# Chunked attention and a softplus FFN on one core: the first four blocks' q and k read in runs of 8 tokens and turned by 64x64 products, with a new order of tasks

## The chip, the cores and the metric

One core of one Trainium2 chip runs the whole program. The metric is the device time of one execution in microseconds. Three executions of the kernel before give a median of 824.95 us (824.27 to 824.95).

## The reference

The inputs q, k, v have the shape (8 batches, 8 heads, 576 tokens, 64) in float32; w_in (512 x 2048) and w_out (2048 x 512) are stored in 8 bytes an element. Attention runs inside chunks of 64 tokens; the heads are then joined into 4608 rows of 512 and go through a two-layer network with softplus.

```
scores = scale * np.matmul(q_c, k_c.transpose(0, 1, 2, 4, 3))   # per chunk of 64 tokens
scores = scores - np.max(scores, axis=-1, keepdims=True)
attn = np.exp(scores)
attn = attn / (np.sum(attn, axis=-1, keepdims=True) + 1e-09)
out = np.matmul(attn, v_c)
...
x = np.ascontiguousarray(attn_out.transpose(0, 2, 1, 3)).reshape(B * S, H * D)
h = x @ w_in
g = np.maximum(h, 0.0) + np.log1p(np.exp(-np.abs(h)))
return (g @ w_out).astype(np.float32)
```

## The kernel before

The tokens are cut into 36 blocks of 128 tokens (two chunks, all 8 heads) and into 9 groups of 512 tokens (four blocks). The program treats the groups in two ways. The first three go straight through: GEMM1 with w_in, softplus, GEMM2 with w_out. The other six go in pairs through a scheme with fewer products (`product`, `mix`, `f_product`); that part begins at about 310 us, and the change leaves its code alone.

Each matrix product is made of three float32r products: a high and a low part of each operand, without low times low. So every weight tile is decoded first. `w_load` brings 512 KB of raw words into one of three buffers, `w_top` and `w_low` take it apart (ScalarE or GpSimd), `w_add` joins the pieces (VectorE), `w_hi` rounds (ScalarE or GpSimd) and `w_lo` subtracts (VectorE or GpSimd). There are 32 such units, called by their number: `w_add3` is the join of unit 3. They are needed one pair per step of GEMM1 and GEMM2 until about 95 us.

The first four blocks (`FIRST_BLK = 4`) open the program, since nothing else can start before their attention. For block i the tasks are, in the names that the planner uses:

- `q{i}`, `k{i}`, `v{i}` (`pe_load`): one DMA each on SyncE's queue; token s goes to partition s, with 8 heads of 64 numbers beside each other, so each piece of 256 bytes is a packet of its own.
- `T{i}` (`pe_t`): 4 transposes of 128x128 for q and 4 for k on TensorE, each with two heads, into two PSUM tiles. `tq{i}` and `tk{i}` copy them to SBUF, both on ScalarE.
- `S{i}` (`pe_s`): scores, 16 products of 64x64; rows and output of one head lie in the same half of the partitions, and heads alternate between the halves.
- `max{i}` on VectorE, `sub{i}` on TensorE (`pe_sub`: adds minus the maximum into PSUM by one product with 512 columns), `exp{i}` on ScalarE, `den{i}` on VectorE (three instructions), `norm{i}` on VectorE, or on GpSimd for blocks 0 and 3.
- `E{i}` transposes the result (4 transposes), `ec{i}` copies it, `V{i}` multiplies by v, `xh{i}` (ScalarE) and `xl{i}` (VectorE) split it into the high and low part of x.

GEMM1 of the first two steps is cut in halves: `G1_a0` and `G1_a1` use blocks 0 and 1, `G1_0` and `G1_1` blocks 2 and 3. With these come `spa0` (softplus), `hia0`, `loa0`, `G2_a0` and so on. Later blocks run as bursts between the GEMM steps; their q and k are loaded in other layouts and turned on VectorE (`blk_t4`, tasks `Uq4`, `Tq4`, ...).

TensorE is kept busy while it waits by filler products of the identity with itself (`keep_warm`); their number comes from the gap that the planner expects. The order of work is made in two steps. `Plan.order` makes a schedule from costs, due times and pool sizes. `Plan.emit` takes each engine's list from it, moves tasks to other engines (`MOVED`), puts single tasks behind others (`BEHIND`), and writes out the program. Each engine then works through its own list in that order, and stalls where the next instruction's input isn't there. A DMA that is issued is an instruction in its queue's list too.

Of the kernel before, what the change touches and what calls it, by code (L numbers as in the profile page):

```python
# [33 lines left out]
class Plan:  # L34
# [108 lines left out]
            raise ValueError(f"never ready: {[n for n in T if n not in fin][:12]}")  # L143
        return out, fin

    def emit(self, moved=(), behind=(), around=lambda t: t["fn"]()):
        T, out = self.tasks, self.order()[0]
        start, lanes, gaps, last = {}, {}, {}, 0.0
        for now, t in out:
# [5 lines left out]
        for name, change in moved:  # L155
            if "eng" in change:
                lanes[T[name]["eng"]].remove(name)
                lanes[change["eng"]].append(name)
            T[name].update(change)
        for name, other in behind:  # L160
            lane = lanes[T[name]["eng"]]
            lane.remove(name)
            lane.insert(lane.index(other) + 1, name)
            gaps[name] = gaps[other] = 0.0
# [27 lines left out]
def chunked_attention_softplus_ffn(  # L192
# [193 lines left out]
    def hd(t):  # L386
        return t.rearrange("p (h d) -> p h d", d=D)
# [39 lines left out]
    def pe_t(i):  # L427
        if i < 2:
            tq, tk = (po_tile(n) for n in range(2))
        else:  # L430
            pa = pa_tile()
            tq, tk = pa[:, 0, :], pa[:, 1, :]
        keep_warm(tq)
        for dst, n in ((tq, 0), (tk, 1)):
            src = hd(slot(i, n))
            for hp in range(HP):
                nc.tensor.transpose(
                    dst[:, hp * P : (hp + 1) * P], src[:, 2 * hp : 2 * hp + 2, :], ident
                )
        live["t", i] = tq, tk  # L440

    def pe_tq(i):
        nc.scalar.copy(slot(i, 3), live["t", i][0])

    def pe_tk(i):
        copy = nc.scalar.copy if i not in TK else nc.vector.tensor_copy
        copy(slot(i, 4), live["t", i][1])

    def pe_s(i):
# [182 lines left out]

    def att_norm(i):
        e, den = live["e", i], live.pop(("den", i))
        (nc.gpsimd if i in NORM_POOL else nc.vector).tensor_tensor(
            e, e, den.unsqueeze(3).to_broadcast(list(e.shape)), op=ALU.mult
        )

# [447 lines left out]

    SOLO = {"a0": 1, "a1": 2}
    HALVED = {"a0": (0, 0), "0": (0, 1), "a1": (1, 0), "1": (1, 1)}
    MOVED = [("w_hi1", {"eng": "ACT"}), ("lo0", {"eng": "DVE"}), ("lo1", {"eng": "DVE"}), ("G1_a0", {"take": []}), ("G1_a1", {"take": []})]
    for fc in range(2):  # L1090
        a, b = f"a{fc}", str(fc)
        MOVED += [(f"sp{a}", {"take": [("u", [f"lo{a}", f"lo{b}"])]}), (f"sp{b}", {"take": []})]
        MOVED += [(f"hi{a}", {"take": [("g", [f"G2_{a}", f"G2_{b}"])]}), (f"hi{b}", {"take": []})]
    BEHIND = (
# [7 lines left out]
    )  # L1102
    plan = Plan(raw=RAW_BUFS, top=TOP_BUFS, low=LOW_BUFS, po0=1, po1=1, po2=1, po3=1, pa=2, g=LAG + 1, u=1,
                ws=1, out0=1, out1=1, out2=1, out3=1, ring0=1, ring1=1, ring2=1, other0=1, other1=1, other2=1, uu0=1, uu1=1, ux0=1, ux1=1)
# [611 lines left out]
                reason="one engine at a time on the memory port",  # L1716
            )

    plan.emit(MOVED, BEHIND, in_turn)


# [32 lines left out]
```

## Time and profile before

| | |
|---|---|
| three executions | 824.95 us median, 824.27 to 824.95 |
| the profiled execution | 824.5 us |
| its span, first to last instruction | 822.7 us |
| TensorE busy | 811.7 us, 99% of the span |
| VectorE busy | 566.0 us, 69% |
| ScalarE busy | 390.9 us, 48% |
| GpSimd busy | 406.3 us, 49% |

All times in the rows are microseconds from the start of the span, unless ns is marked. PE is TensorE, DVE is VectorE, ACT is ScalarE, POOL is GpSimd, SPq is SyncE's queue. A float32 product stands in the trace as two instructions (passes), a transpose or a float32r product as one: `x32` at line 459 are the 16 products of one `S`. The profiled execution took 0.45 us less than the median of the three.

### The profile page before, as it was taken

The numbers are of one execution on the slowest core, as the hardware profiler recorded it, in microseconds if no ns is written. First come the engines' busy times: TensorE is split into PE (matmuls) and PEld (weight loads), VectorE is DVE, ScalarE is ACT, GpSimd is POOL, SyncE is SP. The second block draws the span as 40 slices with busy tenths as digits, with TensorE's granted clock in tenths as the row PEclk, the third lists the DMA queues.
The fourth block names the chain that finished last, engine by engine and source line by source line (L and its number), as shares of the span: only waits on it lengthen the run. The fifth ranks groups of instructions, "written<-read, shape, count | busy, mean of one in ns | idle before, by whom it ended". The sixth has DMA issues, their size and how long they took to land.

```text
span 822.7 us, 16614 instructions
## 1 busy us (share of the span) xinstructions
PE 811.7 (99%) x6186; PEld 686.3 (83%) x6186; DVE 566.0 (69%) x914; ACT 390.9 (48%) x635; POOL 406.3 (49%) x512
## 2 busy tenths in 40 slices
PE   9999999999999999999999999999999999999997
PEld 7787888888888888888888777888888887999997
DVE  3998985357556687386779787376784635798773
ACT  4877765444543574354346444363541424443431
POOL 1555569686987743868856564337204550000000
PEclk9999999999999999999999999999999999999999
DMA  9887767763474456899897499896529999963421
GB/s 217 241 213 199 210 161 220 222 155 112 87 192 124 110 153 215 224 261 253 213 228 186 111 340 288 230 246 209 178 95 315 330 329 342 388 224 115 144 78 52
DMA packets 216483, 168.90 MB, mean 205 GB/s; under 512 B 153937, under 2 KB 186705, under 8 KB 215505
## 3 DMA queue, kind: packets, MB, share of 16 engines
q1 hardware_dynamic: 201648, 117.75, 49.7%
q0 software_dynamic: 14208, 49.56, 20.0%
q8 instruction: 49, 0.80, 0.4%
q10 hardware_dynamic: 544, 0.52, 0.2%
q14 instruction: 34, 0.27, 0.1%
HBM read 115.87 MB, written 50.86 MB: 203 GB/s over the span
## 4 chain that ended last, share of the span: by engine, by line
PE 74%; DMA 10%; DVE 6%; ACT 3%; POOL 3%; issue 3%; SPq 1%; DVEq 0%; ACTq 0%; POOLq 0%
PE po L917 25%; PE pa L858 16%; PE pa L685 13%; PE pa L1060 8%; PE po L1060 6%; DMA spill<-ends 3%; PE pa L648 2%; PE pa L560 1%; DMA raw<-spill 1%; PE po L858 1%; DVE wib L884 1%; DMA xb<-scratch 1%; DMA raw<-in_q_dram 1%; DMA raw<-in_moe_w_out_dram 1%; DVE wib L340 1%
## 5 line engine op out<-in xcount | busy, mean ns | idle before, releaser
L917 PE MATMUL po<-late,g_hi 128*128 128x512 f32 x360 | 110.4, 393 | 0.0
L858 PE MATMUL pa<-wib,xb 128*128 128x512 f32 x360 | 86.8, 394 | 0.7 <-DMA xb<-scratch 0.5
L858 PEld LDWEIGHTS pa<-wib,xb 128*128 128x128 f32 x360 | 66.0, 188 | 19.2 <-ACT wib L864 3.4
L917 PEld LDWEIGHTS po<-late,g_hi 128*128 128x128 f32 x360 | 66.7, 188 | 14.6 <-DVE late L371 0.4
L858 PE MATMUL pa<-wi_hi,xb 128*128 128x512 f32 x240 | 74.3, 390 | 0.8 <-ACT wib L864 0.6
L917 PE MATMUL po<-wo_hi,g_hi 128*128 128x512 f32 x192 | 72.1, 394 | 0.0
L917 PE MATMUL po<-wo_hi,g_lo 128*128 128x512 f32 x192 | 71.4, 391 | 0.2 <-DVE g_lo L709 0.2
L917 PE MATMUL po<-wo_lo,g_hi 128*128 128x512 f32 x192 | 71.2, 390 | 0.0
L917 PE MATMUL po<-late,g_lo 128*128 128x512 f32 x192 | 70.9, 389 | 0.0
L701 ACT ACTIVATE u<-pa 128x512 f32<-128x512 f32 (+1 forms) x48 | 28.3, 589 | 82.1 <-PE pa L685 76.4
L813 POOL DMA_DIRECT2D xb<-scratch x58 | 36.0, 621 | 59.2 <-PE pa L858 57.7
L884 DVE TENSOR_TENSOR wib<-wib,pa 128x512 f32<-128x512 f32 x64 | 44.0, 688 | 26.9 <-PE pa L858 14.5
L892 ACT ACTIVATE ends<-pa 128x512 f32<-128x512 f32 x40 | 23.9, 599 | 76.8 <-PE pa L858 32.2
L858 PEld LDWEIGHTS pa<-wi_hi,xb 128*128 128x128 f32 x240 | 45.0, 188 | 10.9 <-ACT wib L864 1.1
L884 POOL TENSOR_TENSOR wib<-wib 128x512 f32<-128x512 f32 x32 | 42.0, 1312 | 19.5 <-ACT wib L864 19.0
L584 DVE STREAM_TRANSPOSE eT<-qe 32x256 f32<-32x256 f32 x112 | 48.8, 436 | 2.6
L884 DVE TENSOR_TENSOR wib<-pa,wib 128x512 f32<-128x512 f32 x24 | 16.6, 692 | 49.1 <-ACT ends L892 31.4
L864 ACT COPY wib<-pa 128x512 f32<-128x512 f32 x52 | 28.7, 587 | 40.9 <-PE pa L858 40.9
L685 PE MATMUL pa<-xb,wib 128*128 128x512 f32 x192 | 46.5, 390 | 0.3 <-DVE wib L371 0.2
L858 PE MATMUL pa<-wi_lo,xb 128*128 128x512 f32 x120 | 46.7, 389 | 0.0
L709 POOL TENSOR_TENSOR g_lo<-u,g_hi 128x512 fp32r<-128x512 f32 x23 | 31.0, 1348 | 24.7 <-ACT g_hi L705 21.9
L917 PEld LDWEIGHTS po<-wo_hi,g_lo 128*128 128x128 f32 x192 | 36.0, 188 | 8.6 <-DVE g_lo L709 1.1
(370 smaller groups left out, 2078.0 us busy)
## 6 DMA issues: line engine op xcount, KB each, us to landing
xb<-scratch POOLq DMA_DIRECT2D x38, 512.0 KB, 5.4
spill<-ends SPq DMA_DIRECT2D x35, 512.0 KB, 4.8
xb<-scratch POOLq DMA_DIRECT2D x20, 768.0 KB, 6.5
ends<-spill SPq DMA_DIRECT2D x21, 512.0 KB, 3.3
out_dram<-raw SPq DMA_DIRECT2D x34, 256.0 KB, 3.5
raw<-in_moe_w_in_dram SPq DMA_DIRECT2D x16, 512.0 KB, 5.0
raw<-in_moe_w_out_dram SPq DMA_DIRECT2D x16, 512.0 KB, 4.6
scratch<-ends SPq DMA_DIRECT2D x16, 512.0 KB, 2.9
```

Source lines behind the costliest of these rows:

```text
L584: nc.vector.transpose(live["eT", i][d : d + BL, tb], e[s : s + BL, 1 - tb])
L648: nc.tensor.matmul(pa[o, a, col : col + C], vt[r, 4 * j + 2 * h2 + c2, :], eT[r, :, 4 * c2 + 2 * j + h2, :], start=True, stop=True,)
L685: nc.tensor.matmul(ph, wt[:, c, :], x[:, ts_, c, :], start=(n == 0), stop=(n == 3 * KC - 1))
L701: nc.scalar.activation(w["u"], w["ph"], AF.Softplus)
L709: (nc.gpsimd if pool else nc.vector).tensor_tensor(w["lo"], w["u"], w["hi"].bitcast(F32), op=ALU.subtract)
L813: on("ring").dma_start(to[:, here], src[:, cut])
L858: nc.tensor.matmul(w["bank"][BANK[k]], wts[:, q, c, :], x[:, c, :], start=k < NX and c + n == 0, stop=c == 1 and n == 2, skip_group_check= ...
L864: nc.scalar.copy(tmp_of(n), w["bank"][n])
L884: (nc.gpsimd if what in MIX_POOL and w["s"] < LAST else nc.vector).tensor_tensor(out, a, b, op=op)
L892: nc.scalar.activation(u_tiles(j)[i], src, AF.Softplus)
L917: nc.tensor.matmul(pos[w["m"]][t], terms[n][0][:, j * P : (j + 1) * P], terms[n][1], start=(w["first"] and n == 0), stop=n == 2 and w["last"],
L1060: nc.tensor.matmul(f_bank(k)[:, t * HW : (t + 1) * HW], x[:, t * P : (t + 1) * P], wt, start=j == n == t == 0, stop=j == 7 and n == 2 and ...
```

## The change

It has four parts.

1. Loads. For q and k of the first four blocks, 8 tokens of one head that follow each other (2048 bytes) become one piece on one partition. A partition holds one head and one group of 8 tokens; even heads lie in partitions 0 to 63, odd heads in 64 to 127, and within a half the group index is outermost. Each load becomes two DMAs of 64 partitions. All of k0 to k3 is issued by ScalarE, q0 to q3 by SyncE.
2. Turning. For each of the 8 token offsets in a run and each half, one plain 64x64 product of the data with the identity writes 64 columns that lie 8 apart in the PSUM tile: 16 products for q and 16 for k of a block, in place of 4 and 4 transposes.
3. Engines. `tk0`, `tk1`, `norm0` and the subtractions `sub0`, `sub1` go to VectorE (the subtractions then write the result to SBUF).
4. Order. The five engines' opening lists are written out (`FIRST`), with 6 filler products ahead of `T0` (`WARM`) and 1 ahead of `S0`. The list `BEHIND` is another one. On TensorE nothing behind `G1_4` changes except two steps of GEMM1 at about 120 us, which now stand ahead of two steps of GEMM2; ScalarE, VectorE and GpSimd have single tasks swapped with a neighbour over the whole run.

```diff
 def pe_load(eng, i, src, n):
+    if n < 2:
+        (_, rows, b, s0), = rows_of(i)
+        for h2 in range(2):
+            eng.dma_start(
+                slot(i, n)[h2 * C : (h2 + 1) * C],
+                src[b, h2::2, s0 : s0 + rows, :].rearrange("h (g r) d -> g h (r d)", r=RUN),
+            )
+        return
...
     for dst, n in ((tq, 0), (tk, 1)):
-        src = hd(slot(i, n))
-        for hp in range(HP):
-            nc.tensor.transpose(
-                dst[:, hp * P : (hp + 1) * P], src[:, 2 * hp : 2 * hp + 2, :], ident
-            )
+        src = slot(i, n).rearrange("p (r d) -> p r d", r=RUN)
+        dst = dst.rearrange("p (h g r) -> p g h r", h=HP, r=RUN)
+        for run in range(RUN):
+            for a in range(2):
+                r = slice(a * C, (a + 1) * C)
+                nc.tensor.matmul(dst[r, :, :, run], src[r, run, :], ident[r, r], start=True, stop=True)
...
+    MOVED = [("w_hi1", {"eng": "ACT"})] + [(n, {"eng": "DVE"}) for n in ("lo0", "lo1", "tk0", "tk1", "norm0")]
+    MOVED += [(f"sub{i}", {"eng": "DVE", "fn": partial(att_sub, i)}) for i in range(2)]
+    MOVED += [(f"S{i}", {"take": [(f"po{2 + i}", [f"sub{i}"])]}) for i in range(2)]
+    MOVED += [(f"k{i}", {"eng": "ACT", "fn": partial(pe_load, nc.scalar, i, k, 1)}) for i in range(FIRST_BLK)]
...
+        "PE": (
+            "T0 S0 T1 T2 S1 E0 S2 T3 V0 sub2 E1 S3 V1 sub3 E2 G1_a0 V2 G1_a1 E3 V3 G2_a0 G1_0 G1_1 G2_a1 G2_0 "
+            "G1_2 G2_1 G1_3 G2_2 G1_4"
+        ).split(),
...
+    WARM = {"T0": 2.35, "S0": 0.9}
```

TensorE, from the program's start, before (line 418 fillers, 437 `T`, 459 `S`, 616 `sub`, 470 `E`):

```order
L418 MATMUL po_136<-ident 128x128 x15
L437 MATMUL po_136<-ident,late 128x128 x4
L437 MATMUL po_137<-ident,late 128x128 x4
L418 MATMUL po_171<-ident 128x128 x3
L459 MATMUL po_171<-late 64x64 x16
L437 MATMUL po_193<-ident,late 128x128 x4
L437 MATMUL po_194<-ident,late 128x128 x4
L616 MATMUL po_171<-mx,minus 128x512
L459 MATMUL po_210<-late 64x64 x16
```

and of the change (431 fillers, 453 `T`, 473 `S`, 484 `E`):

```order
L431 MATMUL po_135<-ident 128x128 x6
L453 MATMUL po_135<-ident,late 64x16x4 x16
L453 MATMUL po_136<-ident,late 64x16x4 x16
L431 MATMUL po_191<-ident 128x128
L473 MATMUL po_191<-late 64x64 x16
L453 MATMUL po_209<-ident,late 64x16x4 x16
L453 MATMUL po_210<-ident,late 64x16x4 x16
L453 MATMUL pa<-ident,late 64x16x4 x32
L473 MATMUL po_288<-late 64x64 x16
L484 MATMUL po_315<-ident,late 128x128 x4
```

Nine fillers and two `sub` are gone, and `T1` and `T2` stand between `S0` and `S1`.

VectorE, from the program's start, before (605 `max`, 628 to 630 `den`):

```order
L283 MEMSET ends 128x1024
L605 TENSOR_REDUCE mx<-po_171 128x8
L628 TENSOR_REDUCE den<-late 128x8
L629 TENSOR_SCALAR den<-den 128x8
L630 RECIPROCAL den<-den 128x8
L605 TENSOR_REDUCE mx<-po_210 128x8
```

and of the change (461 `tk`, 619 `max`, 624 `sub`, 642 to 644 `den`, 649 `norm`, 345 `w_add`):

```order
L288 MEMSET ends 128x1024
L461 COPY late<-po_136 128x512
L619 TENSOR_REDUCE mx<-po_191 128x8
L624 TENSOR_TENSOR late<-po_191,mx 128x512
L461 COPY late<-po_210 128x512
L642 TENSOR_REDUCE den<-late 128x8
L643 TENSOR_SCALAR den<-den 128x8
L644 RECIPROCAL den<-den 128x8
L649 TENSOR_TENSOR late<-late,den 128x512
L619 TENSOR_REDUCE mx<-po_288 128x8
L624 TENSOR_TENSOR late<-po_288,mx 128x512
L345 ISA wib<-wib,ends 128x1024
```

Five tasks have come in among the first two blocks' work, and `w_add0` moved ahead of `max2`.

SyncE's queue, from the program's start, before:

```order
L398 DMA late_117<-in_q_dram 128x8x64
L398 DMA late_118<-in_k_dram 128x8x64
L398 DMA late_124<-in_q_dram 128x8x64
L398 DMA late_125<-in_k_dram 128x8x64
L398 DMA xa_104<-in_q_dram 128x8x64
L398 DMA xa_104<-in_k_dram 128x8x64
L398 DMA late_161<-in_q_dram 128x8x64
L398 DMA late_162<-in_k_dram 128x8x64
L398 DMA late_126<-in_v_dram 128x8x64
L312 DMA raw0_191<-in_moe_w_in_dram 128x4x512
```

and of the change:

```order
L404 DMA late_117<-in_q_dram 64x1x512 x2
L404 DMA late_126<-in_q_dram 64x1x512 x2
L404 DMA late_175<-in_q_dram 64x1x512 x2
L404 DMA xa_104<-in_q_dram 64x1x512 x2
L411 DMA late_119<-in_v_dram 128x8x64
L411 DMA late_128<-in_v_dram 128x8x64
L317 DMA raw0_307<-in_moe_w_in_dram 128x4x512
L317 DMA raw1_320<-in_moe_w_in_dram 128x4x512
L322 DMA raw2_322<-in_moe_w_out_dram 128x2048
```

The loads of k are gone from this queue (ScalarE issues them: six DMAs as its first work, two more behind `tq1`), and three weight loads stand behind the first two v; before, it was one load behind one v.

## Rows read from the trace of the kernel before

**Rows 1.** The page: busy time of each engine, its share of the span and its instructions.

```profile
PE 811.7 (99%) x6186; PEld 686.3 (83%) x6186; DVE 566.0 (69%) x914; ACT 390.9 (48%) x635; POOL 406.3 (49%) x512
```

**Rows 2.** Busy time by stretch: the stretch, its length, then for PE, PEld, DVE, ACT and POOL the busy time and in brackets the instructions, then the granted clock of the throttle (PEclk), the DMA share and GB/s.

```profile
25.00:30.00 5.00, 4.77 (x91) 4.38 (x92) 4.31 (x6) 4.46 (x8) 3.48 (x4) 1.00 1.01 236
...
36.00:82.00 46.00, 45.24 (x377) 36.59 (x377) 41.25 (x69) 34.13 (x56) 24.84 (x24) 1.00 0.79 207
...
100.00:120.00 20.00, 20.00 (x208) 16.59 (x207) 16.63 (x25) 13.99 (x24) 13.33 (x13) 1.00 0.70 192
```

**Rows 3.** The timeline of TensorE from 0 to 36 us: start, length, engine, line, operation, tiles, shape and count; in brackets the idle time before it and what ended it.

```profile
1.35 6.17 PE L418 MATMUL po<-ident 128*128 128x128 f32 x30 [1.35 <-POOL ident masks.py:199]
7.36 1.04 PE L437 MATMUL po<-ident,late 128*128 128x128 f32 x8
8.24 0.83 PE L418 MATMUL po<-ident 128*128 128x128 f32 x6
9.13 1.15 PE L459 MATMUL po<-late 64*64 64x64 f32 x32
...
11.16 1.10 PE L616 MATMUL po<-mx,minus 128*128 128x512 f32 x2
12.19 1.15 PE L459 MATMUL po<-late 64*64 64x64 f32 x32
13.27 1.09 PE L437 MATMUL pa<-ident,xa 128*128 128x128 f32 x8
14.20 1.04 PE L437 MATMUL pa<-ident,late 128*128 128x128 f32 x8
15.07 1.02 PE L616 MATMUL po<-mx,minus 128*128 128x512 f32 x2
15.93 0.60 PE L470 MATMUL po<-ident,late 128*128 128x128 f32 x4
16.50 1.15 PE L459 MATMUL po<-late 64*64 64x64 f32 x32
17.48 1.10 PE L459 MATMUL po<-ka,qe 64*64 64x64 f32 x32
...
22.17 0.94 PE L418 MATMUL po<-ident 128*128 128x128 f32 x6
24.33 0.65 PE L470 MATMUL po<-ident,late 128*128 128x128 f32 x4 [1.23 <-DVE late L635]
25.23 0.66 PE L470 MATMUL po<-ident,xa 128*128 128x128 f32 x4 [0.25 <-POOL xa L635]
25.64 0.72 PE L685 MATMUL po<-xb,wi_hi 128*128 128x256 f32 x4
...
27.87 0.71 PE L418 MATMUL pa<-ident 128*128 128x128 f32 x4
28.51 0.69 PE L486 MATMUL pa<-late 64*64 64x64 f32 x32
...
30.82 0.71 PE L685 MATMUL pa<-xb,wi_hi 128*128 128x256 f32 x4
```

**Rows 4.** The filler's line (418) in two stretches: engine, operation, count, then the duration of one in ns (least, median, most) and the first and last start.

```profile
L418 PE MATMUL po<-ident x7: 421/421/421, 3.6 to 4.9; 128*128 128x128 f32 x7
...
L418 PE MATMUL po<-ident x5: 274/275/275, 6.8 to 7.3; 128*128 128x128 f32 x5
```

**Rows 5.** SyncE's queue: the issues of q0 and k0 (start, length), and k0's time from issue to landing in us.

```profile
0.72 0.43 SPq L398 DMA_DIRECT2D late<-in_q_dram  x1
1.21 0.57 SPq L398 DMA_DIRECT2D late<-in_k_dram  x1
...
late<-in_k_dram SPq DMA_DIRECT2D x1, 256.0 KB, 4.0
```

**Rows 6.** What all DMA engines moved in 0 to 30 us, in GB/s by 40 equal slices.

```profile
GB/s 0 0 55 240 286 199 235 232 215 222 217 217 218 217 218 218 227 288 339 274 236 213 227 159 116 365 373 375 346 355 124 27 76 344 289 106 270 235 221 195
```

**Rows 7.** Timelines of ScalarE and VectorE: the load of the softplus table and a maximum out of PSUM.

```profile
30.12 1.28 ACT L701 ACT_TABLE_LOAD   x1
...
10.32 0.69 DVE L605 TENSOR_REDUCE mx<-po 128x8 f32<-128x512 f32 x1 [8.40 <-PE po L459]
```

**Rows 8.** The timeline of TensorE from 44 to 125 us, at the places where it isn't dense, and one burst later on.

```profile
51.14 0.69 PE L560 MATMUL pa<-ka,qe 64*64 64x64 f32 x32 [0.25 <-ACT u L701]
...
72.24 2.11 PE L685 MATMUL pa<-xb,wib 128*128 128x512 f32 x8 [0.23 <-DVE wib L371]
74.28 0.69 PE L648 MATMUL pa<-eT,xa 64*64 64x64 f32 x32
...
77.82 0.69 PE L560 MATMUL pa<-ka,qe 64*64 64x64 f32 x32 [0.21 <-DVE ka L536]
78.44 1.21 PE L917 MATMUL po<-wo_hi,g_hi 128*128 128x512 f32 x4
...
81.56 3.00 PE L685 MATMUL pa<-xb,wib 128*128 128x512 f32 x12
...
117.42 0.69 PE L648 MATMUL pa<-eT,qk 64*64 64x64 f32 x32
...
119.45 2.11 PE L917 MATMUL po<-late,g_hi 128*128 128x512 f32 x8
```

**Rows 9.** Who TensorE waited for from 82 us to the end, the longest wait: us in total, times, longest.

```profile
PE pa L858 <- ACT wib L864: 0.6, 1, 0.6
```

More of the change, by code (lines that the diff above doesn't have):

```diff
@@ L144, in order, with emit @@
         return out, fin
-    def emit(self, moved=(), behind=(), around=lambda t: t["fn"]()):
+    def emit(self, moved=(), first={}, warm={}, behind=(), around=lambda t: t["fn"]()):
         T, out = self.tasks, self.order()[0]
@@ L159, in emit @@
             T[name].update(change)
+        for eng, names in first.items():
+            lanes[eng] = names + [n for n in lanes[eng] if n not in names]
+            gaps.update(dict.fromkeys(names, 0.0))
+        gaps.update(warm)
         for name, other in behind:
@@ L217, in chunked_attention_softplus_ffn @@
     LAG = 1
+    RUN = 8
     HALF_FC = 8
@@ L445, in pe_tk @@
     def pe_tk(i):
-        copy = nc.scalar.copy if i not in TK else nc.vector.tensor_copy
+        copy = nc.scalar.copy if i > 1 else nc.vector.tensor_copy
         copy(slot(i, 4), live["t", i][1])
@@ L634, in att_norm @@
         e, den = live["e", i], live.pop(("den", i))
-        (nc.gpsimd if i in NORM_POOL else nc.vector).tensor_tensor(
+        (nc.gpsimd if i in NORM_POOL and i else nc.vector).tensor_tensor(
             e, e, den.unsqueeze(3).to_broadcast(list(e.shape)), op=ALU.mult
@@ L691, in shared @@
         fc, n = HALVED[str(w["name"])]
+        if name == "u":
+            fc, n = n, fc
         if n == 0:
@@ L1088, in chunked_attention_softplus_ffn @@
     HALVED = {"a0": (0, 0), "0": (0, 1), "a1": (1, 0), "1": (1, 1)}
-    MOVED = [("w_hi1", {"eng": "ACT"}), ("lo0", {"eng": "DVE"}), ("lo1", {"eng": "DVE"}), ("G1_a0", {"take": []}), ("G1_a1", {"take": []})]
+    MOVED = [("w_hi1", {"eng": "ACT"})] + [(n, {"eng": "DVE"}) for n in ("lo0", "lo1", "tk0", "tk1", "norm0")]
+    MOVED += [(f"sub{i}", {"eng": "DVE", "fn": partial(att_sub, i)}) for i in range(2)]
+    MOVED += [(f"S{i}", {"take": [(f"po{2 + i}", [f"sub{i}"])]}) for i in range(2)]
+    MOVED += [(f"k{i}", {"eng": "ACT", "fn": partial(pe_load, nc.scalar, i, k, 1)}) for i in range(FIRST_BLK)]
     for fc in range(2):
-        a, b = f"a{fc}", str(fc)
-        MOVED += [(f"sp{a}", {"take": [("u", [f"lo{a}", f"lo{b}"])]}), (f"sp{b}", {"take": []})]
-        MOVED += [(f"hi{a}", {"take": [("g", [f"G2_{a}", f"G2_{b}"])]}), (f"hi{b}", {"take": []})]
-    BEHIND = (
[7 rows of a table removed]
+        MOVED.append((f"G1_a{fc}", {"take": [(f"po{1 + fc}", [f"spa{fc}"])]}))
+        MOVED.append((f"hia{fc}", {"take": [("g", [f"G2_a{fc}", f"G2_{fc}"])]}))
+        MOVED.append((f"hi{fc}", {"take": []}))
+        MOVED.append((("spa0", "sp0")[fc], {"take": [("u", [("loa0", "loa1"), ("lo0", "lo1")][fc])]}))
+        MOVED.append((("spa1", "sp1")[fc], {"take": []}))
+    FIRST = {
+        "SP": (
+            "q0 q1 q2 q3 v0 v1 load0 load1 load2 v2 v3 load3 q4 k4 load4 load5 q5 load6 k5 load7 load8 load9 "
+            "load10 v4 load11 v5 load12 load13 q6"
+        ).split(),
+        "PE": (
+            "T0 S0 T1 T2 S1 E0 S2 T3 V0 sub2 E1 S3 V1 sub3 E2 G1_a0 V2 G1_a1 E3 V3 G2_a0 G1_0 G1_1 G2_a1 G2_0 "
+            "G1_2 G2_1 G1_3 G2_2 G1_4"
+        ).split(),
+        "ACT": (
[4 rows of a table added]
+        ).split(),
+        "DVE": (
[3 rows of a table added]
+        ).split(),
+        "POOL": (
+            "w_top0 w_hi0 w_top2 w_hi2 w_top3 norm3 w_lo2 w_hi3 w_hi4 w_lo4 w_lo3 w_hi5 w_hi6 w_hi7 w_top10 "
+            "w_lo8 lo2"
+        ).split(),
+    }
+    WARM = {"T0": 2.35, "S0": 0.9}
+    BEHIND = (
[12 rows of a table added]
     )
@@ L1717, in in_turn @@
             )
-    plan.emit(MOVED, BEHIND, in_turn)
+    plan.emit(MOVED, FIRST, WARM, BEHIND, in_turn)
 _INS = ["q", "k", "v", "moe_w_in", "moe_w_out"]
```

26 rows, old and new, of tables (BEHIND, FIRST) are left out of this document.

## The prediction

> **What bounds the kernel now.** I read the page first: TensorE is busy 99% of the span, the next engine 69% [rows 1]. So a change pays only if it takes time out of TensorE's own row, and the busy time by stretch says where any is left. From 100 to 120 us the row is full; from 36 to 82 us it is busy 45.24 of 46 us [rows 2], and behind 82 us the longest single wait is 0.6 us [rows 9]. The rest lies in the opening, which the timeline shows [rows 3]: 15 fillers run until `T0` at 7.36; then come turns, scores and subtractions, with a filler group and an idle time wherever a block's chain over ScalarE and VectorE isn't done; at 30.82 `G1_0` starts, and the two half steps `G1_a0`, `G1_a1` and all four blocks are behind it. From there work is dense. I therefore compare how early the same amount of TensorE work is done, with 30.82 as the mark, and then ask whether the decode of weights follows.
>
> **The change part by part.** All terms are TensorE's time up to that mark; minus is a gain.
>
> *A, start of `T0`.* Fillers hold it until 7.36, though k0 landed at 1.21 + 4.0 = 5.2 [rows 3, 5]. Now 6 fillers are 12 passes; 7 starts from 3.6 to 4.9 are 0.21 us apart [rows 4], so the fillers end at 1.35 + 12 x 0.21 = 3.9, and the landing decides. q0 and k0 are 0.52 MB. In pieces of 256 bytes the DMA engines move about 217 GB/s, in the slices with weight loads 340 to 375 [rows 6]: 2.4 against 1.5 us. The early slices of before were at up to 286, and k0's issue stood 0.49 us behind q0's. I take a landing at 4.3, 0.9 earlier. Bounds 3.9 (the fillers) and 5.2 (no earlier than before). A = 4.3 - 7.36 = -3.1 (-3.5 to -2.2).
>
> *B, the clock.* The PEclk column reads 1.00 all along [rows 2], but a filler pass takes 421 ns until 4.9 and 274 from 6.8 [rows 4], after TensorE had been busy since 1.35 without a break: its two levels, 1.2 and 2.4 GHz, with the step near 6.6. `T0` will now begin at the low level. If the step stays at 6.6, work from 4.3 to 6.6 goes at half speed: B = +1.15. Bounds: 0 (the step comes by 4.3) and +2.8 (it waits until 10, behind `S0`: half of 5.7).
> The Trainium skill, "TensorE: Matmul & The Clock Gate", Part 1 (the HAM clock gate), says that the low clock is the default, that sustained activity lifts it and idle time brings it back. That speaks against fewer fillers: `T0` follows a gap of some 0.4 us. No row here shows TensorE idle before the step; by the rule B would lie at its upper bound, and the whole sum would be 1.65 worse.
>
> *C, turning.* A turn is 8 passes from 13.27 to 14.20 and 14.20 to 15.07, 0.90 us [rows 3]. The new one is 32 plain products, 64 passes. No row shows this operation. The nearest is `S`: also 64x64 passes in float32, also alternating between the same two quarters of the array: 32 passes from 16.50 to 17.48, 30.6 ns each. So 64 x 30.6 = 1.96 us, and C = 4 x (1.96 - 0.90) = +4.2. Low bound: the bursts, 128 such passes over all four quarters in 119.45 - 117.42 = 2.03 us, 15.9 ns each [rows 8], C = +0.5. High bound: columns that lie 8 apart in PSUM, which no row shows, at twice the price, C = +12.1; I take `S`, which differs from the new turn in nothing else.
>
> *D, two `sub` leave TensorE*: 11.16 to 12.19 and 15.07 to 15.93 [rows 3], D = -1.9. VectorE does them now, at about its 0.69 for 128x512 [rows 7], and `tk0`, `tk1`, `norm0` too: 5 x 0.69 = 3.5 us, beside three products of TensorE. VectorE's first task in before starts at 10.32 after 8.40 idle [rows 7], so that is cover; without it, up to 3.5 us would pass to the blocks' chains.
>
> *E, waits.* Before: 8.24 to 9.13 under fillers, 22.17 to 24.33, 0.25, and 27.87 to 28.51: 3.9 us [rows 3]. After, laid out by hand with these durations in the new order: `T1` and `T2` (3.9 us) fill the time in which block 0 goes through max, sub, exp and den. Left are `S0` behind `tk0` (0.7), `sub3` behind `max3` (0.3), the third part of `G1_a0` behind `xl1`, which has three decode tasks ahead of it (0.4), and `V3` behind `ec3`: on ScalarE that stands behind the table load of 1.28 [rows 7], `spa0`, `w_top4`, `xh2`, `w_low4` and `hia0` (1.1). Together 2.5, E = -1.4. Bounds -3.2 and +1.
>
> Sum to the mark: -3.1 + 1.15 + 4.2 - 1.9 - 1.4 = about **-1.0**.
>
> *F, 36 to 82 us.* TensorE waits 0.25 + 0.23 + 0.21 there; four half bursts from 74.28 to 78.44 take 4.2, against 2.0 at 117.42, 6 fillers included (they remain); and the step from 78.44 takes 3.12, against 2.72 when dense [rows 8]. About 1.9 us hang on decoded weights, q, k and VectorE, which is busy 41 of 46 us [rows 2]. By the layout VectorE is about 2 us ahead of before at the same task (`loa1`), since weight loads 0 to 2 are issued ahead of v2 and v3 and the small packets no longer fill the DMA engines until 12 us. If it stays ahead of TensorE, which gains 1.0, part of the 1.9 falls away. I take the middle, F = **-1.0** (0 to -1.9).
>
> *At nothing:* the issues of k on ScalarE (six of about 0.43, then its table load, all before `tq0`); k3's two issues under `T2`; the new `BEHIND` list, since TensorE is dense behind 82 us (bound -2 if its waits vanish, +1 if a swap makes one).
>
> Total -2.0: span 820.7. The profiled execution took 824.5 for a span of 822.7, 1.8 more, and lay 0.45 under the median: 820.7 + 1.8 + 0.45 = **823.0**.
>
> **The rivals.**
> 1. *The step of the clock comes late* (B). For it: fewer fillers, gaps before and behind `T0`. Against: 2.6 us of fillers and a full `T0` lie ahead of 6.6. Until 10 us it costs 1.65 more: 824.6, no change; slower only beyond 14.
> 2. *Slower: the strided write into PSUM makes a pass dearer* (C). There are 256 passes, so each 10 ns cost 2.6 us. From 45 ns a pass (+3.7) the kernel is slower than before by the bound below; at 61 ns it takes 830.8. For it: no row has such a write. Against: each pass still writes 64 numbers per partition.
> 3. *Slower: VectorE and ScalarE become the opening's bound* (D and E). Their lists are fixed; one late input holds the decode behind it. If the waits of E grow to 5.2 us in place of 2.5 and the gain of F is lost, that is 3.7 more: 826.7, from where it counts as slower.
> 4. *The decode stage gives back all it can*: F -1.9, the fillers' end and a landing at 3.9 (A -3.5, B +1.35), E -2.4: 820.9. For it: the weights are issued earlier. Against: the layout of E already lets everything follow at once.
> 5. *k on the other queue does nothing.* The Trainium skill, "DMA: Bandwidth & Descriptors" (Issuing engines are not separate DMA queues), says that such a split saves only the time of issue. Rows show that time as 0.49 us; with a landing at 5.2, A is -2.2 and B +0.7, and the time is 823.4.
>
> **How the numbers follow.** The median of three executions has a spread under 0.1%; I call 0.2% (1.65 us, 823.3) what can be told from no change. Forecast 0.42, its own range 821.8 to 824.2, so 0.24 of it faster and 0.18 the same. Rival 4: 0.24, faster. Rival 1: 0.15, 0.10 the same and 0.05 slower. Rivals 2 and 3: 0.08 each, slower. Rival 5: 0.03, the same. Faster 0.48, same 0.31, slower 0.21. The range 820.0 to 827.0 leaves out the low tail of C and most of rivals 2 and 3 above 827.
>
> **What would show it.** `T0` starts near 4.3; the passes of its line (453) are 60 ns apart at first, 31 later, and `T1` takes 2.0 us; `S0` starts near 8.3; `G2_a0` starts near 29.8 with the four blocks done; the step that began at 81.56 begins near 79.6, and from there the rows run parallel. A first step of the clock behind 8 us, a `T1` over 2.8 us, or TensorE idle for more than 3 us between 20 and 36 would prove me wrong, each at its own term.

## The result, and the profile after

The changed kernel takes **833.02 us** (median of 5 runs, 829.59 to 834.65) against 824.95 for the kernel before: ratio 1.0096, 95% interval 1.0067 to 1.0125. It is slower by some 8 us, outside the range of the prediction. The profiled execution took 834.65 us with a span of 832.9, 10.2 more than before.

First the page: busy time of the engines, and the queue on which programs arrive (packets, MB, share of 16 engines' span).

```profile
PE 813.0 (98%) x6374; PEld 688.5 (83%) x6374; DVE 565.3 (68%) x919; ACT 389.5 (47%) x633; POOL 402.5 (48%) x511
...
q8 instruction: 50, 0.82, 0.4%
```

Against [rows 1] TensorE has 188 passes more but only 1.3 us more busy time. So most of the 10.2 us is time in which it did nothing. The opening, on TensorE's timeline (columns as in [rows 3]):

```profile
1.34 2.93 PE L431 MATMUL po<-ident 128*128 128x128 f32 x12 [1.34 <-POOL ident masks.py:199]
4.20 0.47 PE L453 MATMUL po<-ident,late 64*64 64x64 f32 x2
6.26 2.08 PE L453 MATMUL po<-ident,late 64*64 64x64 f32 x62 [1.59 <-DMA late<-in_q_dram]
...
9.22 1.15 PE L473 MATMUL po<-late 64*64 64x64 f32 x32 [0.46 <-DVE late L461]
10.17 2.06 PE L453 MATMUL po<-ident,late 64*64 64x64 f32 x64
12.04 1.60 PE L453 MATMUL pa<-ident,late 64*64 64x64 f32 x48
13.91 0.68 PE L453 MATMUL pa<-ident,late 64*64 64x64 f32 x16 [0.28 <-issue]
...
18.82 0.33 PE L453 MATMUL pa<-ident,xa 64*64 64x64 f32 x2 [0.70 <-DMA xa<-in_k_dram]
20.16 1.34 PE L453 MATMUL pa<-ident,xa 64*64 64x64 f32 x29 [1.01 <-DMA xa<-in_k_dram]
...
22.05 2.07 PE L630 MATMUL po<-mx,minus 128*128 128x512 f32 x2
...
29.98 0.74 PE L699 MATMUL po<-xb,wi_hi 128*128 128x256 f32 x4 [0.46 <-DVE xb L679]
...
34.15 0.69 PE L500 MATMUL pa<-xa,eT 64*64 64x64 f32 x32 [0.73 <-ACT xa L488]
34.77 0.73 PE L933 MATMUL po<-wo_hi,g_hi 128*128 128x512 f32 x2
...
83.11 1.20 PE L933 MATMUL po<-wo_hi,g_hi 128*128 128x512 f32 x4
```

Two passes of `T0` start at 4.20, since q's lower half is there; its upper half comes at 6.26. The passes are 32 ns apart, `T1` takes 1.9 us. `T3` waits twice for k3, and the `sub2` behind it takes 2.07 us where a `sub` took 1.1 [rows 3]. The mark (the place where the four blocks and both half steps are done, here the start of `G2_a0`) comes at 34.77, 3.95 us later than 30.82; the GEMM2 step that began at 78.44 [rows 8] begins at 83.11, 4.67 later. Why k3 is late, on ScalarE's timeline with its queue (ACTq), and in the list of issues (count, size, median us to landing):

```profile
0.73 4.49 ACTq L404 DMA_DIRECT2D late<-in_k_dram  x6
5.25 1.28 ACT L457 ACT_TABLE_LOAD   x1 [5.25 <-DMA late<-in_k_dram]
...
11.86 0.55 ACTq L404 DMA_DIRECT2D xa<-in_k_dram  x1
...
12.45 0.70 ACTq L404 DMA_DIRECT2D xa<-in_k_dram  x1
```

```profile
xa<-in_k_dram ACTq DMA_DIRECT2D x2, 128.0 KB, 7.3
```

k3 is issued at 11.86, behind `exp0`, which waited 3.8 us for VectorE, and then takes 7.3 us to land. The stretches behind this wait and behind one near 577 us (columns as in [rows 2]), and that place on the timeline:

```profile
21.00:26.00 5.00, 5.00 (x91) 3.41 (x91) 1.75 (x4) 3.14 (x6) 0.00 (x0) 0.66 0.75 193
...
576.00:581.00 5.00, 1.95 (x9) 1.50 (x8) 1.72 (x3) 0.00 (x0) 3.42 (x6) 1.00 1.03 351
581.00:586.00 5.00, 5.00 (x16) 3.97 (x16) 2.67 (x7) 3.52 (x5) 0.62 (x1) 0.66 0.13 36
```

```profile
574.61 0.65 PE L574 MATMUL pa<-ka,qe 64*64 64x64 f32 x32
...
576.69 0.62 PE L933 MATMUL po<-late,g_hi 128*128 128x512 f32 x2
580.35 0.40 PE L933 MATMUL po<-late,g_lo 128*128 128x512 f32 x1 [3.05 <-issue]
...
582.26 1.06 PE L874 MATMUL pa<-wi_hi,xb 128*128 128x512 f32 x2
```

In the middle of a GEMM2 step TensorE stands still for 3.05 us, and nothing in the profile releases it ("issue"). The granted clock of the five microseconds behind is 0.66: part of them is at the lower level (1.2 GHz), which costs 5 x 0.34 = 1.7 us. The same holds for 21 to 26 us. Before, the longest wait behind 82 us was 0.6 [rows 9]. Last, who TensorE waited for from 690 to 730 us:

```profile
PE pa L1076 <- DVE ka L1059: 1.4, 1, 1.4
PE pa L1076 <- DVE xb L1059: 0.7, 1, 0.7
```

So of the 10.2 us 4.7 are there by 83 us, 4.8 arise near 577 and 2.7 near 710 (2.1 of them these two waits); between, 1.0 comes back ahead of 577 and 0.9 behind it.

### The profile page after: what moved, and what is told of

Read it like the earlier page. It is cut to its first block, busy times and chain, and to the rows that moved or that the text cites. A ratio compares the mean times of both kernels' runs of the same rounds, so it can differ in the third digit from the quotient of the medians.

```text
span 832.9 us, 16984 instructions
## 1 busy us (share of the span) xinstructions
PE 813.0 (98%) x6374; PEld 688.5 (83%) x6374; DVE 565.3 (68%) x919; ACT 389.5 (47%) x633; POOL 402.5 (48%) x511
## 4 chain that ended last, share of the span: by engine, by line
PE 82%; DMA 7%; DVE 5%; ACT 2%; issue 2%; POOL 1%; SPq 0%; DVEq 0%; ACTq 0%; POOLq 0%
PE po L933 28%; PE pa L874 21%; PE pa L699 13%; PE pa L1076 7%; PE po L1076 5%; PE po L874 3%; DMA spill<-ends 2%; PE pa L662 2%; PE pa L574 2%; DMA xb<-scratch 1%; DMA raw<-in_moe_w_in_dram 1%; DMA xa<-in_k_dram 1%; DMA ends<-spill 1%; DVE wib L345 1%; DMA late<-in_q_dram 1%
## 5 line engine op out<-in xcount | busy, mean ns | idle before, releaser
L900 DVE TENSOR_TENSOR wib<-wib,pa 128x512 f32<-128x512 f32 x64 | 44.0, 687 | 29.3 <-PE pa L874 16.4
L699 PEld LDWEIGHTS pa<-xb,wib 128*128 128x128 f32 x192 | 36.0, 188 | 8.2 <-DVE wib L376 0.8
```

Source lines behind the costliest of these rows:

```text
L699: nc.tensor.matmul(ph, wt[:, c, :], x[:, ts_, c, :], start=(n == 0), stop=(n == 3 * KC - 1))
L900: (nc.gpsimd if what in MIX_POOL and w["s"] < LAST else nc.vector).tensor_tensor(out, a, b, op=op)
```

## The experiments

Each ratio is to the kernel before, timed beside the run on the same chip; its median there was 823.6 to 824.1 us, so compare two runs by their ratios. The first four take the change apart.

**e1, k3 issued earlier.**

```diff
-            "k0 k1 k2 tq0 exp0 tq1 k3 tk2 ...
+            "k0 k1 k2 k3 tq0 exp0 tq1 tk2 ...
```

> The changed kernel with k3's two DMAs issued fourth on ScalarE's queue, ahead of the table load, in place of behind exp0 and tq1. Theory O (the opening loses the time: T3 waits 1.7 us for k3, and the clock falls to its lower level right behind that wait for 3.4 us, worth about 1.7 us more): both are gone, the mark G2_a0 comes at 31 to 32 us in place of 34.77, and the time is 829 to 830 against 833.0 of the changed kernel. Rival L (the later order loses it): the mark comes earlier, but the stages behind give the gain back and the time stays at 832 to 834.

833.79 us, ratio 1.0129 (1.0106 to 1.0152): no gain. The wait for k3 is gone, and others take its place:

```profile
6.10 3.67 PE L453 MATMUL po<-ident,late 64*64 64x64 f32 x62 [1.42 <-DMA late<-in_q_dram]
...
15.89 0.68 PE L453 MATMUL pa<-ident,late 64*64 64x64 f32 x16 [0.83 <-issue]
...
22.41 0.80 PE L453 MATMUL pa<-ident,xa 64*64 64x64 f32 x20 [1.97 <-issue]
```

`T0` took 3.67 us in place of 2.08, 59 ns a pass: the clock stepped up at 9.8 us here and at 4.7 in the profile of the changed kernel, with the same instructions ahead. And `T2` and `T3` now wait for nothing that the profile shows. Theory O named the wait rightly and its effect wrongly. The time is in rival L's range, but not for its reason: the mark comes later (36.50), not earlier.

**e2, the layout alone**: the new loads and products in the kernel before, with its order and queues.

```diff
-                nc.tensor.transpose(
-                    dst[:, hp * P : (hp + 1) * P], src[:, 2 * hp : 2 * hp + 2, :], ident
-                )
+                    nc.tensor.matmul(dst[r, :, :, run], src[r, run, :], ident[r, r], start=True, stop=True)
```

> The kernel before, in its own order and on its own queues, with the new loads (runs of 8 tokens, 2048 bytes each) and the 64 turning products for each of the first four blocks. Theory T (the turning is dear and the longer runs land no earlier): four times 1.1 us of TensorE work more, T0 at 6 to 7.4 us as before: 827 to 829.5 against 825. Rival O: the layout alone costs little, since TensorE waited in the opening anyway, 824 to 826. Rival L: 824 to 826 as well, and then only the run with the new later order is slow.

828.96 us, ratio 1.0071 (1.0058 to 1.0084). Its turns, on TensorE's timeline:

```profile
7.64 2.08 PE L449 MATMUL po<-ident,late 64*64 64x64 f32 x64
...
17.37 1.80 PE L449 MATMUL pa<-ident,late 64*64 64x64 f32 x56
19.93 0.45 PE L449 MATMUL pa<-ident,late 64*64 64x64 f32 x8 [0.76 <-issue]
20.31 1.12 PE L626 MATMUL po<-mx,minus 128*128 128x512 f32 x2
```

The second `sub` starts at 20.31 against 15.07 [rows 3]: 5.2 us for four turns, of which 0.76 is again a wait without a releaser and 0.28 the later `T0`. Theory T holds: the turning costs what its passes take, and nothing in the opening pays for it.

**e3, the late moves alone**, 37 of the new `BEHIND` in the kernel before (two shown).

```diff
-        ... ("sub29", "xs1_0"), ("Tq28", "Te26"), ...
+        ... ("w_hi29", "w_top30"), ("sp14", "w_hi29"), ...
```

> The kernel before with its own opening, loads and first table, but with the moves of the new table that concern tasks after some 300 us in place of its own late moves (37 moves). Theory L (the later order costs 2 us in the final passes, and up to 6 with the stall near 577 us): 827 to 831 against 825. Theories O and T: within 1 us of 825, and no stall near 577 us.

824.25 us, ratio 1.0009 (0.9997 to 1.0021). In the profiled execution they lose 1.7 us from 697 to 719, 1.2 of it in waits for the same two tiles, and win 2.9 between 411 and 498. Theory L falls, and the wait at 577 isn't there.

**e4, the new order with the old layout.**

```diff
-        if n < 2:
-            (_, rows, b, s0), = rows_of(i)
...
-                    nc.tensor.matmul(dst[r, :, :, run], src[r, run, :], ident[r, r], start=True, stop=True)
+                nc.tensor.transpose(
+                    dst[:, hp * P : (hp + 1) * P], src[:, 2 * hp : 2 * hp + 2, :], ident
+                )
```

> The changed kernel with the old loads (256-byte rows) and the eight 128x128 transposes for each block, in the new order and with k still on ScalarE's queue. Theory T: four times 1.1 us of TensorE work less, T0 within 1 us of that of the changed kernel: 828 to 830 against 833.0. Theory O: k3 is still late and the clock still falls, so what the products save is waited for: 831.5 to 833.5. Theory L: 832 to 833.5.

825.16 us, ratio 1.0020 (1.0007 to 1.0033): everything but the layout costs 1.6 us, and by the two ratios (1.0096 and 1.0020) the layout costs 6.3 in the new order. That is more than theory T said, so it does something besides its 4.2 us of products. (The two medians alone say little of what arises only where layout and order meet: 0.71% for the layout by itself and 0.20% for the rest add up to 0.91%, against 0.96%, each with an interval of 0.1 to 0.3% to either side.) Its `T0`, and two waits that the order brings:

```profile
4.67 1.32 PE L442 MATMUL po<-ident,late 128*128 128x128 f32 x8 [0.40 <-DMA late<-in_q_dram]
...
17.61 0.69 PE L491 MATMUL pa<-late 64*64 64x64 f32 x32 [2.04 <-ACT late L479]
...
31.77 0.69 PE L491 MATMUL pa<-xa,eT 64*64 64x64 f32 x32 [1.77 <-ACT xa L479]
```

With rows of 256 bytes all of q0 is there by 4.67, earlier than the upper half in runs of 2048 bytes.

**A new theory, I.** TensorE's program is itself brought by DMA: 50 packets, 0.82 MB, 16.4 KB each. The Trainium skill, "Perfetto Trace Analysis" (The 4-stage abstract model), says that an instruction has 64 bytes. The changed program has 6374 passes, each with a weight load, and 137 other instructions in the trace, together 12,885, which at 64 bytes is 0.82 MB, so row and page agree: 256 instructions, some 128 passes, a piece. (From e4 with 6150 passes to e5 with 6454 the packets go from 48 to 51.) Counted in program order, the instructions that waited longest without a releaser are these (number, and its rest when divided by 256; another start of the count shifts all alike):

```text
changed kernel   0.28 us:  453, 197   3.05 us: 9668, 196
e1               0.83 us:  453, 197   1.97 us:  709, 197   2.2 us: 9668, 196
e2               0.76 us:  709, 197
e5               2.26 us:  708, 196
e7               2.48 us:  709, 197   2.8 us: 9668, 196
e9               2.37 us: 9412, 196
e10              1.59 us:  709, 197   0.17 us:  965, 197
e13              2.00 us: 9413, 197
```

All stand at the same place of a piece, and so do four shorter waits without a releaser: 0.35 us at 392.74 in the changed kernel, 0.40 at 497.45 in e5, 0.35 at 389.42 in e9, and 0.21 at 496.77 in the kernel before. Each of these 17 waits ended 1.3 to 1.6 us after an instruction packet had come to its end. 64x64 passes 31 ns apart use a piece up in 4 us, the bursts of 128 passes in 2.

**e5, 40 idle products ahead of `T0`.**

```diff
         keep_warm(tq)
+        for _ in range(40 if i == 0 else 0):
+            nc.tensor.matmul(tq[:C, :C], ident[:C, :C], ident[:C, :C], start=True, stop=True)
```

> The changed kernel with 40 idle 64x64 products more between the fillers and T0, 40 x 31 ns = 1.2 us in the 1.6 us in which TensorE waits for q's second half anyway; every later instruction of TensorE stands 40 places further on. Theory I (TensorE's program comes in 16-KB pieces, and it waits where a piece ends shortly after a quick run of small products): the wait of 3.0 us in a GEMM2 near 577 us, and the half clock behind it, go away or move to another line, and the time falls by 3 to 5 us, to 828 to 830. Rival V (the wait near 577 us comes from the v loads that GpSimd issues there): the wait stays on its line, 832 to 834.

833.45 us, ratio 1.0106 (1.0083 to 1.0130). The wait near 577 is gone in the profiled execution (829.73 us), where 497 to 592 us took 5 us less. But a product in float32 is two passes, and passes that all use one quarter of the array follow each other at 61 ns, not 31:

```profile
4.21 4.88 PE L448 MATMUL po<-ident 64*64 64x64 f32 x79
...
19.94 0.21 PE L475 MATMUL po<-late 64*64 64x64 f32 x1 [2.26 <-issue]
```

The opening lost 2.3 us by 37 us, of which 0.7 are left at 118, and the median does not show the theory's gain: by the time alone rival V would stand.

**e6, k on ScalarE's queue, old layout, 6 fillers**, in the kernel before.

```diff
+    MOVED += [(f"k{i}", {"eng": "ACT", "fn": partial(pe_load, nc.scalar, i, k, 1)}) for i in range(FIRST_BLK)]
...
-    plan.emit(MOVED, BEHIND, in_turn)
+    plan.emit(MOVED, BEHIND, [f"k{i}" for i in range(FIRST_BLK)], {"T0": 2.35}, in_turn)
```

> The kernel before, with its own layout, transposes and order, and two edits only: k0 to k3 are issued first on ScalarE's queue, and 6 fillers stand ahead of T0 in place of 15. Theory Q (with 256-byte rows and k on a second queue both operands land by 4.7 us, as in the run with the old layout): T0 starts at 4.7 in place of 7.36, the opening keeps 1 to 2.7 us of it, 821 to 823 against 823.6. Rival D (the decode stage is bound by the weights and gives all back): 823.6 within 0.8. Rival S (ScalarE's queue delays tq0 behind the DMA issues and the table load): 824 to 826.

823.23 us, ratio 0.9994 (0.9981 to 1.0008). `T0` starts at 4.53, but `S0` waits 1.89 us for ScalarE's copy, since the table load stands behind four issues: of 2.8 us 0.7 are left at `S0`. That is the wait that rival S named, but the time is rival D's:

```profile
8.41 1.15 PE L464 MATMUL po<-late 64*64 64x64 f32 x32 [1.89 <-ACT late L452]
```

**e7, each half on its own queue**: q and k's lower 64 partitions by SyncE, the upper by ScalarE.

```diff
-            for h2 in range(2):
+            for m, x in enumerate(SOURCES):
                 eng.dma_start(
-                    slot(i, n)[h2 * C : (h2 + 1) * C],
+                    slot(i, m)[n * C : (n + 1) * C],
```

> The changed kernel with the two halves of each q and k split over the two queues (SyncE the lower 64 partitions of q and of k, ScalarE the upper) in place of q on one and k on the other. Theory H (the second half of q is late because its DMA is issued second on the same queue, a second later): q is whole by 4.7 to 5 us, T0 starts 1.2 to 1.6 us earlier than 6.26, and the time falls by about that, 831 to 832. Rival R (the 2048-byte packets move at some 245 GB/s and q's half lands at 6 whoever issues it): T0 within 0.4 us of 6.2, time 832 to 834.

831.08 us, ratio 1.0074 (1.0050 to 1.0098). Theory H: q is whole by 4.20, 2 us earlier. In exchange k0's two halves, now issued second, landed 3.8 and 4.5 us after it, at 5.2 and 6.0 in place of 3.6 and 4.7. The interval of the ratio overlaps that of the changed kernel, so the gain in time isn't shown. Most of `T0` then ran at the lower clock, and what was a wait for k3 is one for instructions:

```profile
4.20 3.16 PE L454 MATMUL po<-ident,late 64*64 64x64 f32 x64
...
19.71 1.04 PE L454 MATMUL pa<-ident,xa 64*64 64x64 f32 x19 [2.48 <-issue]
```

**e8, e4 with three moves** that take weights out of the way of `ec0`, `exp1` and `ec3`.

```diff
-            "k0 k1 k2 tq0 exp0 tq1 k3 tk2 tq2 w_low0 ec0 exp1 tq3 tk3 ...
+            "k0 k1 k2 k3 tq0 exp0 tq1 tk2 tq2 ec0 exp1 tq3 tk3 w_low0 ...
```

> The run with the old layout in the new order, with three moves: k3 fourth on ScalarE's queue ahead of the table load, w_low0 behind tk3 on ScalarE (ec0 and exp1 stood behind its wait for the first weights, 4.5 us) with w_add0 behind norm1 on VectorE, and w_top4 and w_low4 behind ec3. Theory W (the rest of that run's loss lies in those waits: 2.0 and 1.8 us of TensorE for ec0 and ec3, 0.5 for k3): the mark 2 to 4 us earlier than 32.4 us, time 821 to 823 against 825.2 of that run and 823.6 of the kernel before. Rival D (what the opening gains the decode stage gives back): 824.5 to 825.5.

825.33 us, ratio 1.0014 (1.0000 to 1.0027). The mark comes 2 us earlier than in e4, as theory W said, and 0.3 to 0.5 of that is left by 100 us: rival D.

**e9, half the instructions for the same columns**, on e7; half of the tokens are left unturned.

```diff
-            for run in range(RUN):
+            for run in range(0, RUN, 2):
...
-                    nc.tensor.matmul(dst[r, :, :, run], src[r, run, :], ident[r, r], start=True, stop=True)
+                    nc.tensor.matmul(dst[r, :, :, run : run + 2].rearrange("p g h r -> p r g h"), src[r, run, :], ident[r, r].unsqueeze(1).to_broadcast([C, 2, C]), start=True, stop=True)
```

> The run with the split halves, but each turning product writes 128 columns in place of 64 (one run of tokens to its own columns and to those of the next run, so that half of the tokens are not turned at all): half as many instructions of TensorE for the same columns, 128 passes fewer in all, which is one 16-KB piece of its program. Theory I (pieces of the program arrive too slowly for passes of 31 ns): the wait of 2.5 us in T3 goes, and with it the lower clock behind it, 3 to 4 us in the opening, while the wait of 2.8 us in the GEMM2 near 577 us stays on its line, since every later instruction keeps its place within a piece; 826.5 to 828.5 against 831.1 of the run with split halves. Rival C (the opening's loss is the turned columns themselves, and the wait in T3 is for data): the mark G2_a0 within 1 us of 33.9, time 830 to 832.

828.45 us, ratio 1.0054 (1.0041 to 1.0067): by the two ratios 1.7 less than e7, with intervals that overlap. The wait for instructions in `T3` and the lower clock behind it are gone, though `T3` waited 2.28 us for q3 in their place, so the mark came only 1.7 us earlier than in e7. The wait near 577 stays on its line, as theory I said, one piece earlier in the count. Behind neither wait did the clock fall. Both waits on the timeline, and the stretches behind them (columns as in [rows 2]):

```profile
18.32 2.06 PE L454 MATMUL pa<-ident,xa 64*64 64x128 f32 x29 [2.28 <-DMA xa<-in_q_dram]
...
578.84 0.39 PE L934 MATMUL po<-late,g_lo 128*128 128x512 f32 x1 [2.37 <-issue]
```

```profile
18.00:23.00 5.00, 4.68 (x88) 3.69 (x90) 1.83 (x5) 2.48 (x6) 0.76 (x1) 1.00 0.99 226
579.00:584.00 5.00, 5.00 (x23) 4.12 (x23) 2.25 (x5) 3.53 (x5) 0.27 (x1) 1.00 0.36 100
```

**e10, 26 idle products in three waits** of the changed kernel.

```diff
+    plan.pads = {"S0": 7, "G1_a1": 7, "V3": 12}
```

> The changed kernel with 26 idle 64x64 products more (52 passes of TensorE) in three waits that it has anyway: 7 ahead of S0, 7 ahead of G1_a1, 12 ahead of V3. The run with 40 idle products ahead of T0 lost in the opening what it gained near 577 us, since they took 61 ns a pass and not 31. Theory I: opening within 0.8 us of the changed kernel's, the wait near 577 us gone or below 1 us, 828 to 830 against 833.0. Rival V (the wait belongs to what moves at 577 us): it stays on its line, 832 to 834.

830.68 us, ratio 1.0077 (1.0064 to 1.0090), 828.03 in the profiled execution. The wait and the lower clock near 577 are gone, which gave some 5 us there; the opening was 2 us longer, 1.6 of it `T0` at the lower clock until 9.9 us. That is theory I, but the time is above the 828 to 830 that it named, and the interval overlaps that of the changed kernel.

**e11 and e12, an earlier `T0` in the kernel before**: k0 alone on ScalarE's queue and 6 fillers; and 7 fillers in place of 15 with nothing else.

```diff
+        gaps["T0"] = 2.8
```

> The kernel before with its own layout, transposes and order; k0 alone is issued by ScalarE, ahead of its table load, k1 to k3 stay with SyncE, and 6 fillers stand ahead of T0 in place of 15. The run with all four k on ScalarE started T0 2.8 us earlier but S0 only 0.7, since the table load stood behind four issues. Theory Q: the table is loaded by 2.6 us, S0 starts 2 to 2.5 us earlier than 9.13, and 1.5 to 2.5 us of it remain at the end: 821.5 to 822.5 against 823.8. Rival D (a later stage gives it back): 823 to 824.5.

> The kernel before with one edit: 7 fillers ahead of T0 in place of 15, no queue and no layout changed. Theory Q: k0 lands at 5.2 us (4.0 us after its issue at 1.2), so T0 starts at 5.2 to 5.6 in place of 7.36 and most of it is kept: 822 to 823 against 823.8. Rival B (with fewer fillers the clock steps up later, and T0 and S0 run at half speed): T0 earlier, S1 within 0.5 us of 12.19, 823.5 to 825.

824.49 us, ratio 1.0013 (1.0004 to 1.0023), and 824.21, ratio 1.0004 (0.9995 to 1.0012). Neither gains. The timeline of e12, its waits from 28 to 82 us, and k0's size and time from issue to landing:

```profile
4.50 1.49 PE L438 MATMUL po<-ident,late 128*128 128x128 f32 x8
...
29.59 0.71 PE L686 MATMUL pa<-xb,wi_hi 128*128 128x256 f32 x4 [0.69 <-DVE xb L666]
...
78.70 1.20 PE L918 MATMUL po<-wo_hi,g_hi 128*128 128x512 f32 x4
```

```profile
PE pa L561 <- ACT u L702: 1.4, 1, 1.4
PE pa L686 <- DVE xb L666: 0.7, 1, 0.7
...
late<-in_k_dram SPq DMA_DIRECT2D x1, 256.0 KB, 4.0
```

With one queue and rows of 256 bytes `T0` starts at 4.50 without a wait: fillers alone held it at 7.36. The mark comes 1.2 us earlier, and the step at 78.44 comes at 78.70. So theory Q fails in both. Rival B's time fits e12, but not its reason, since `S1` starts at 9.78, 2.4 us earlier; what happened is rival D of e11: the stage behind the mark takes back all of it.

**e13 and e14, the kernel before with 33 idle products ahead of `E2`, and with 14**, in place of its 6 filler passes.

```diff
-        keep_warm(tp)
+        keep_warm(tp, 33 if i == 2 else 0)    # 14 in e14; this many idle 64x64 products
```

> The kernel before with one edit: the 3 fillers ahead of E2 become 33 idle 64x64 products, 66 passes in place of 6, in the 1.2 us in which TensorE waits for VectorE there and the 0.9 of the fillers. All later instructions of TensorE stand 120 places further on, so that one 16-KB piece of its program ends where it does in the changed kernel, nine passes behind the run of 128 small products at 569.5 us. Theory I: a wait of 2 to 3.5 us that nothing in the profile releases turns up at instruction 197 of a piece in the GEMM2 behind that run, with the lower clock behind it, and the time rises by 2 to 5 us, to 826 to 829 against 824. Rival V (the wait belongs to the changed kernel's v loads or its other order): no such wait, 823.5 to 824.8.

> The same edit with 14 idle products in place of 33, as a control: later instructions stand 44 places further on, and no piece ends within twenty passes behind the run at 569.5 us. Theory I: no wait of over 0.5 us that nothing releases, 823.5 to 824.8 against 824. Rival P (the idle products themselves cost something): between 824 and what the run with 33 gives.

831.59 us, ratio **1.0105** (1.0082 to 1.0128), and 825.32, ratio 1.0023 (1.0010 to 1.0036). In e13:

```profile
580.23 0.65 PE L562 MATMUL pa<-ka,qe 64*64 64x64 f32 x32
...
585.15 0.72 PE L919 MATMUL po<-late,g_hi 128*128 128x512 f32 x2 [2.00 <-issue]
...
585.95 1.02 PE L860 MATMUL pa<-wi_hi,xb 128*128 128x512 f32 x2
```

The wait turns up ten passes behind the burst, at the 197th place of a piece, with the lower clock behind it, in a kernel that has neither the new layout nor the new order; e14 has none. Theory I holds for the wait, and rival V falls. For the times it does not do as well: e13 lies above its 826 to 829, and e14 above its 823.5 to 824.8, where rival P put it, though its profiled execution (824.19) shows no loss. The profiled execution of e13 (836.75, the longest of its six) has two more waits that cost about 4 and 3.5 us, 2.4 us for VectorE's `ka` near 420 and 1.9 for ScalarE's copy near 451, each with the lower clock behind it. Both engines were waiting for DMAs there: VectorE 3.67 us for a load of k that took 7.4 us to land, ScalarE 3.12 us for a transfer of the output out of its buffer, against 1.04 in the kernel before. Why these took longer is not settled. The products themselves took 4.0 us in place of 2.1, and the new wait, with its lower clock, cost 3.9.

## Why the prediction was wrong, point by point

The reading that TensorE's idle time lies in the opening was right, but e11 and e12 show that a gain there is worth nothing: what is won ahead of 30.82 is taken back by 78 us. (In the profiled execution of e6 1.7 us were left at 78; its time doesn't show them.)

- **A failed** (-3.1, its worst bound -2.2; measured -1.1). "The landing decides" was right, "a landing at 4.3, 0.9 earlier" was not: the upper half of q, second on its queue, came at 6.26. The prediction took the start of `T0` for the landing of both q and k; but `T0` turns q first, and in e12, with the old loads, it began at 4.50 while k0 landed at 5.25, just as the rows said (1.21 + 4.0). So the old loads were there no later than the new ones. Rival 5 had this half right. The Trainium skill, "DMA: Bandwidth & Descriptors" (Issuing engines are not separate DMA queues), says that a second issuing engine saves the time of issue only. The runs agree, and show not even that: k0 took 4.0 us from its issue at 1.21 behind q0 (e12), and 4.6 us from its issue at 0.72 on ScalarE's queue (e11).
- **B** (+1.15) was 0 in the profile of the changed kernel and +1.6 in e1 and e10: the step came at 4.7, 9.8 and 9.9 us. Bounds right, the middle a matter of the execution.
- **C** (+4.2) held: the passes are 31 to 32 ns apart, e2 lost 5.2 with its 0.76 of waiting and a `T0` 0.28 later. Rival 2 falls.
- **D** (-1.9) held for TensorE: the two `sub` are gone. VectorE was not free cover, though: `exp0` waited 3.8 us for it, and k3's issue stood behind `exp0`.
- **E failed** (waits of 2.5 us, -1.4). From 8.27 us to the mark they are 4.5, with the fillers counted, and the lower clock behind `T3` adds 1.7. The step was "at nothing: k3's two issues under `T2`": k3 took 7.3 us to land. With that wait away (e1, e7) the fetch of instructions stands behind it, 2.0 to 2.5 us, and the clock falls in both.
- Sum to the mark: -1.1 + 0 + 4.2 - 1.9 + 0.6 + 1.7 = +3.5, with +3.95 measured and -1.0 predicted.
- **F failed** (-1.0; measured +0.7 from the mark to the step at 83.11). A gain is given back there, as e8 and e12 show; a loss is not made good.
- **"At nothing: the new `BEHIND` list" failed** in what it looked at. The list costs 2.7 us near 710 in the changed kernel (1.7 in e3) and wins about as much elsewhere (e3: within 0.2%). What cost 4.8 us behind 82 us in the profiled execution, 3.05 and 1.8 of clock, was the 188 passes that the prediction priced by their duration only. (The same wait cost 4.6 us in e7, but 2.4 in e1 and 2.6 in e9, where the clock did not fall.) They moved every later instruction, so that a piece of TensorE's program began with a burst of 128 passes and was used up before the next had come. e13 put the kernel before at that place; the same wait and the same lower clock came, and the time rose by as much as the whole change cost, though not by that wait alone.

Not one of the rivals named the fetch of instructions. Why the next piece came late just there is open. Its packet began 4.7 us after TensorE had passed the last border between pieces; at 420 us, where a piece was used up in 3 us, the packet began 0.5 us before the border, and nothing waited. What sets this is not shown: in 578 to 580.4 us the DMA engines were full, but they were in other stretches too. That all executions have the wait, and so its share of the median's 8 us, isn't shown either: it is in four profiled ones, of the changed kernel, e1, e7 and e9, and not in e5 and e10, which idle products shift and whose medians gained 1.6 us at most.

No run beats the kernel before; e3, e6 and e12 equal it.

## What to carry to other kernels

Price a rewritten step by its instructions as well as by its work: here TensorE's program came in pieces of 256 instructions, and some 190 small passes more made it wait for the next piece in the opening, and moved a later piece so that it waited far away from the edit. A wait that names no releaser and stands at the same place of a piece in several kernels points to that; shift it with idle passes before blaming the order around it. Before an opening is made shorter, delete fillers or work from it and see whether the next stage keeps the gain.

## What the hardware showed

- A stall at the end of a piece lasted until the instruction packet had landed and 1.3 to 1.6 us more, in all 17: one packet moved from 578.1 to 579.0 us, TensorE went on at 580.35; from 19.7 to 21.0 in e1, it went on at 22.41.
- The lower clock followed waits of 1.7 us (in two parts), 2.0 and 3.0 us; the granted clock of five microseconds behind each is 0.66 (changed kernel, e1, e13). Behind others as long it did not come: 1.89 us ahead of `S0` in e6, 2.23 near 581 in e1, 2.28 and 2.37 in e9. So the length of one wait does not tell whether the clock falls.
- The first step up of the clock came between 4.4 and 9.9 us in the profiles of kernels whose openings begin alike.
- Idle 64x64 passes in one quarter of the array follow each other at 61 ns at the higher clock (e5, e13), those that alternate between two quarters at 31.
